# Queries and keys transposed in 32x32 blocks by VectorE, weighing of e moved to GpSimd

## The chip, the cores and the metric

The kernel runs on one core of a Trainium2 chip. The metric is the device time of one execution in microseconds (us). The times shown are those of three runs; the profile is that of one further execution, whose own time stands beside its span.

## What is computed

The reference is an attention with a causal window of 128 tokens and a linear bias, followed by a gated feed-forward layer with a short convolution over the tokens. All arrays are float32.

```python
batch, n_heads, seq, head_dim = (8, 8, 576, 64)          # q, k, v
d_model, d_ff, kernel = 512, 1024, 3

scores = scale * np.matmul(q, k.transpose(0, 1, 3, 2))   # scale 1/8
bias = slopes[:, None, None] * (-np.abs(rel))[None, :, :]
mask = (rel >= 0) & (rel < window)
scores = np.where(mask, scores + bias[None], -1000000000.0)
attn = np.exp(scores - np.max(scores, axis=-1, keepdims=True))
attn = attn / (np.sum(attn, axis=-1, keepdims=True) + 1e-09)
attn_out = np.matmul(attn, v)

x = attn_out, heads side by side, as (8, 576, 512)
h = np.maximum(x @ w_in, 0.0)
conv_out[:, s] = sum over k of conv_w[k] * h[:, s + k - 1]     # zeros outside a sequence
gate = 1.0 / (1.0 + np.exp(-conv_out))
return h * gate @ w_out
```

## The kernel before

The 8 x 576 = 4608 tokens are cut into 36 tiles of 128 tokens, t = 0 to 35, without regard to the ends of the sequences: sequence b begins at token 576b, so a boundary falls at the edge of a tile (tiles 9, 18, 27) or in its middle (tiles 4, 13, 22, 31). The eight heads are taken in two halves u = 0, 1 of four heads (HU).

For a tile, the attention half goes through these steps (the short names are those of the order lists):

- LD: two DMAs (one per piece, where a tile lies in two sequences) bring queries and keys, tokens on partitions, into `rqk`; LV does so for the values, into `rv`. All DMAs are issued by SP's queue.
- Q: TensorE transposes `rqk` in eight 128x128 blocks into PSUM (`pt`, L245); QO: ScalarE copies them to `qkT_all` (L250), which holds three tiles.
- S.u: TensorE makes the scores of a half (`sc`, L287); MA.u.a: VectorE merges, masks and adds the bias, and writes `e` (L308, L316, L319); RM.u: the row maximum (L323).
- X.u.h: ScalarE takes the exponentials of two heads, with their sums (L328).
- N.u: VectorE takes the reciprocal of the sums (L339, L340) and multiplies e by it (L341, one instruction of 128x512).
- T.u: TensorE transposes e into `pa` (L348); RL.u: ScalarE copies it to `rl` (L353); SEL.u: GpSimd cuts it into the side of this tile and that of the tile before (L359, L362).
- AV: TensorE multiplies with the values (L379); XH, XL, XF: the result as a high and a low part in `x` (L390, L394, L408, L410).

The feed-forward half works on chunks of 256 tokens, four steps s to a chunk, two steps to each tile's period: UH (L423, twelve matmuls into `p`), HH (relu, L431), Z and CV (the convolution: L437 on ScalarE, L450 on VectorE), TH (L457), GT (L461), GH (L468), GL (GpSimd, L473), D (L487, twelve matmuls into `o`), OB (store). Where a chunk holds the boundary of two sequences, each CV takes four VectorE instructions in place of two.

The order on every engine is written out by hand: `OPENING` for tiles 0 to 5 with the loading and splitting of the weights (F, CL, RS, V, H, P, W), then `PERIOD` once for each t from 6 to 35, then `TAIL`. A name with a number i in PERIOD means tile t + i or step s + i. Every engine runs its instructions in the order in which the list names them, and waits where an input or a buffer is not ready. The PERIOD of before:

```
S0.0 MA0.0.0 S0.1 GH-1 AV-1 LV2 XH-1 MA0.0.1 XL-1 RM0.0 D-2 OB-2 X0.0.0 X0.0.1 XF-1 UH0.0 HH0.0
MA0.1.0 Z0.0 UH0.1 HH0.1 MA0.1.1 GL-1 UH1.0 RM0.1 X0.1.0 CV0.0 N0.0 Z0.1 UH1.1 T0.0 X0.1.1 HH1.0
CV0.1 TH0 RL0.0 N0.1 HH1.1 Q1 LD3 GT0 SEL0.0 Z1.0 QO1 CV1.0 T0.1 Z1.1 RL0.1 CV1.1 GH0 SEL0.1 TH1 GT1
GL0 D-1 OB-1
```

PSUM for `pt`, `sc`, `pa`, `av` and `p` comes from one pool of five buffers in rotation.

Of the kernel before, what the change touches and what calls it, by code (L numbers as in the profile page):

```python
# [21 lines left out]
def tile_alibi_window_attention_conv_glu(  # L22
# [103 lines left out]

# [108 lines left out]
    def fetch(t, dst, src):  # L235
        for r, b, s, n in segments(t):
            nc.sync.dma_start(out=dst[r : r + n], in_=src[b, :, s : s + n, :].rearrange("h s d -> s h d"))

    def qkT(t, u):
        rqk = raws[t][0]  # L240
        ps = pst.tile([P, 2, NG, P], F32, name=f"pt{t}_{u}", tag="tr")
        for i in range(2):
            for g in range(NG):
                h = u * HU + 2 * g
                nc.tensor.transpose(ps[:, i, g, :], rqk[:, i, h : h + 2, :].rearrange("p h d -> p (h d)"), ident)  # L245
# [91 lines left out]
    def normal(t, u):  # L337
        e, st, pss = sms.pop((t, u))
        nc.vector.tensor_scalar(out=st[:, 2, :], in0=st[:, 1, :], scalar1=1e-9, scalar2=None, op0=ALU.add)  # L339
        nc.vector.reciprocal(out=st[:, 2, :], in_=st[:, 2, :])  # L340
        nc.vector.tensor_tensor(out=e, in0=e, in1=st[:, 2, :].unsqueeze(2).to_broadcast([P, HU, P]), op=ALU.mult)  # L341
        es[t, u] = e

    def attnT(t, u):
        e = es.pop((t, u))
        ps = pst.tile([P, HU, P], F32, name=f"pa{t}_{u}", tag="tr")
        for j in range(HU):
            nc.tensor.transpose(ps[:, j, :], e[:, j, :], ident)  # L348
# [167 lines left out]


# [93 lines left out]
```

## Time and profile before

| | us |
|---|---|
| median of three runs (lowest, highest) | 673.04 (672.59, 673.32) |
| the profiled execution, its own time | 672.56 |
| its span | 670.5 |
| busy: TensorE matmuls, VectorE, ScalarE, GpSimd | 633.5, 514.1, 450.6, 192.5 |

The span is the time from the first to the last record of the profiled execution; the 2.1 us around it belong to its time too. The periodic part (t = 6 to 35) begins at 111.65 us, and the last period begins at 603.71 us. Most periods whose steps hold no boundary take 16.7 us, those that hold one about 17.4 us; three short ones, after a tile that begins a sequence, take 15.8 us.

### The profile page before, as it was taken

What the parts mean: (1) busy time and instruction counts of PE and PEld (TensorE: products, weight loads), DVE (VectorE), ACT (ScalarE), POOL (GpSimd) and SP (SyncE); (2) the same over time, 40 slices, a digit from 0 to 9 for tenths busy, and PEclk for the clock granted to TensorE, in tenths of its full rate; (3) what the DMA queues carried; (4) which work ended last, traced back from release to release, by engine and by line L of the source; (5) the groups of instructions that cost most, each with busy time, mean ns of one, the idle gap of its engine ahead of it and who ended that gap; (6) DMA issues with size and microseconds to landing.
All of it is one profiled execution on the core that took longest, in us unless ns stands there. A gap on an engine that the chain in (4) does not pass through costs nothing.

```text
span 670.5 us, 15774 instructions
## 1 busy us (share of the span) xinstructions
PE 633.5 (94%) x6097; PEld 552.6 (82%) x6097; DVE 514.1 (77%) x1225; ACT 450.6 (67%) x1275; POOL 192.5 (29%) x235
## 2 busy tenths in 40 slices
PE   4679899999999999999999999999999999999996
PEld 3357678988898889888999999988898889888994
DVE  7988997777877788777877788777877888777341
ACT  3768776676767676667676767666776667666452
POOL 2242323332232233223233333322232223223221
PEclk9789999999999999999999999999999999999998
DMA  8753721222222222232502222223232322000000
GB/s 231 199 169 98 171 48 39 57 67 54 73 48 68 61 64 65 48 79 49 126 32 50 80 48 79 50 48 81 48 80 48 81 48 79 18 32 1 32 32 31
DMA packets 120109, 47.16 MB, mean 70 GB/s; under 512 B 113356, under 2 KB 113380, under 8 KB 120036
## 3 DMA queue, kind: packets, MB, share of 16 engines
q1 hardware_dynamic: 120036, 46.17, 26.8%
q8 instruction: 48, 0.79, 0.5%
q14 instruction: 25, 0.20, 0.1%
HBM read 36.72 MB, written 9.44 MB: 69 GB/s over the span
## 4 chain that ended last, share of the span: by engine, by line
PE 67%; DVE 18%; issue 6%; ACT 5%; POOL 2%; DMA 1%; POOLq 0%; SPq 0%; DVEq 0%; ACTq 0%
PE o L487 24%; PE p L423 20%; PE av L379 8%; DVE zp L450 7%; PE sc L287 7%; PE pa L348 4%; PE pt L245 3%; DVE e L341 3%; ACT zp L437 2%; PE pw L200 1%; POOL gl L473 1%; DVE wg L184 1%; DVE z L461 1%; DVE sc L316 1%; DVE wg L181 1%
## 5 line engine op out<-in xcount | busy, mean ns | idle before, releaser
L450 DVE SCALAR_TENSOR_TENSOR zp<-hh,cw,zp 128x256 f32<-128x256 f32 (+7 forms) x384 | 162.0, 422 | 81.6 <-ACT zp L437 72.7
L423 PEld LDWEIGHTS p<-x,wi 128*128 128x128 f32 x1728 | 212.3, 189 | 8.6 <-PE o L487 4.0
L423 PE MATMUL p<-x,wi 128*128 128x258 f32 x1728 | 215.2, 283 | 2.8 <-DVE x L408 2.8
L487 PE MATMUL o<-wo,gh 128*128 128x512 f32 x576 | 188.0, 407 | 1.5 <-ACT gh L468 1.5
L328 ACT ACTIVATE e<-e,st 128x128 f32<-128x128 f32 x288 | 112.1, 391 | 55.4 <-DVE st L323 55.4
L359 POOL TENSOR_SCALAR_AFFINE_SELECT rl<-rl 128x512 f32<-128x512 f32 x64 | 41.4, 647 | 344.5 <-ACT rl L353 344.5
L487 PEld LDWEIGHTS o<-wo,gh 128*128 128x128 f32 x576 | 103.6, 189 | 27.7 <-issue 5.1
L487 PE MATMUL o<-wo,gl 128*128 128x512 f32 x288 | 114.9, 399 | 0.6 <-POOL gl L473 0.6
L473 POOL TENSOR_TENSOR gl<-z,gh 128x512 fp32r<-128x512 f32 x72 | 92.3, 1282 | 53.6 <-ACT gh L468 52.8
L431 ACT ACTIVATE hh<-p 128x258 f32<-128x258 f32 x144 | 55.1, 383 | 45.2 <-PE p L423 45.2
L437 ACT ACTIVATE zp<-hh,cw 128x256 f32<-128x256 f32 x144 | 68.7, 477 | 22.0 <-DVE zp L450 13.7
L461 DVE SCALAR_TENSOR_TENSOR z<-zp,hh 128x512 f32<-128x512 f32 x72 | 49.5, 688 | 28.5 <-ACT zp L457 28.5
L379 PE MATMUL av<-rl,rv 128*64 128x128 f32 x1088 | 69.1, 280 | 1.9 <-POOL rl L362 1.1
L487 PEld LDWEIGHTS o<-wo,gl 128*128 128x128 f32 x288 | 54.5, 189 | 14.2 <-POOL gl L473 1.1
L379 PEld LDWEIGHTS av<-rl,rv 128*64 128x64 f32 x1088 | 60.2, 139 | 6.9 <-issue 3.0
L287 PEld LDWEIGHTS sc<-qkT_all 64*64 64x64 f32 x1792 | 51.7, 136 | 16.8 <-issue 4.7
L319 DVE SCALAR_TENSOR_TENSOR e<-sc,bias 128x256 f32<-128x256 f32 x144 | 61.2, 425 | 4.9
L308 DVE COPY_PREDICATED sc<-m_same,sc 128x256 f32<-128x256 uint8 x144 | 60.5, 420 | 4.9 <-PE sc L287 4.8
L457 ACT ACTIVATE zp<-zp 128x512 f32<-128x512 f32 x72 | 41.9, 582 | 30.2 <-DVE zp L450 18.2
L348 PE MATMUL pa<-ident_r,e 128*128 128x128 f32 x288 | 44.8, 279 | 17.4 <-DVE e L341 12.9
L287 PE MATMUL sc<-qkT_all 64*64 64x128 f32 (+2 forms) x1792 | 59.0, 270 | 2.2 <-DVE e L319 0.8
L362 POOL TENSOR_SCALAR_AFFINE_SELECT rl<-rl 128x512 f32<-128x512 f32 x72 | 46.3, 643 | 48.7 <-ACT rl L353 37.0
(65 smaller groups left out, 626.3 us busy)
## 6 DMA issues: line engine op xcount, KB each, us to landing
out_dram<-ob SPq DMA_DIRECT2D x36, 256.0 KB, 2.2
rqk<-in_q_dram SPq DMA_DIRECT2D x32, 256.0 KB, 3.6
rqk<-in_k_dram SPq DMA_DIRECT2D x32, 256.0 KB, 3.9
rv<-in_v_dram SPq DMA_DIRECT2D x32, 256.0 KB, 3.2
wst<-in_moe_w_in_dram SPq DMA_DIRECT2D x8, 512.0 KB, 5.5
wst<-in_moe_w_out_dram SPq DMA_DIRECT2D x8, 512.0 KB, 4.0
rqk<-in_q_dram SPq DMA_DIRECT2D x8, 128.0 KB, 3.3
rqk<-in_k_dram SPq DMA_DIRECT2D x8, 128.0 KB, 3.6
```

Of the source, the lines that this page charges most:

```text
L287: nc.tensor.matmul(strip(pss[a][qs, g, :], [to for to, _ in run]), qkT_all[rows, 0, u, g, base + c * QW : base + (c + 1) * QW], strip(qkT_ ...
L308: nc.vector.copy_predicated(out=s_all.rearrange("p g (c w) -> p g c w", w=QW), mask=m_same.rearrange("p (c w) -> p c w", w=QW).unsqueeze(1 ...
L319: nc.vector.scalar_tensor_tensor(out=heads, in0=s_all, scalar=-0.125, in1=b, op0=ALU.mult, op1=ALU.add)
L328: nc.scalar.activation(out=e[:, j, :], in_=e[:, j, :], func=AF.Exp, bias=st[:, 0, j : j + 1], scale=-1.0, accum_out=st[:, 1, j : j + 1],)
L348: nc.tensor.transpose(ps[:, j, :], e[:, j, :], ident)
L379: nc.tensor.matmul(ps[a * D : (a + 1) * D, u * NG + g], vraw[tt][:, u * HU + j], rl[:, side, j], start=n == 0, stop=n == len(sides) - 1,)
L423: nc.tensor.matmul(ps[:, :XW], a[:, cc, f * P : (f + 1) * P], x[:, cc, :], start=n == 0, stop=n == last)
L437: nc.scalar.activation(out=zps[s][:, ff, :], in_=hhs[s][:, ff, 1 : 1 + CW], func=AF.Copy, scale=cw[:, 1, f : f + 1])
L450: nc.vector.scalar_tensor_tensor(out=z[:, ff, a:cut], in0=hh[:, ff, a + kk : cut + kk], scalar=cw[:, kk, f : f + 1], in1=z[:, ff, a:cut], ...
L461: nc.vector.scalar_tensor_tensor(out=zgs[s], in0=zps.pop(s), scalar=1.0, in1=hhs.pop(s)[:, :, 1 : 1 + CW], op0=ALU.add, op1=ALU.mult)
L473: nc.gpsimd.tensor_tensor(out=gl, in0=zgs.pop(s), in1=as32(gh), op=ALU.subtract)
L487: nc.tensor.matmul(oos[c][m], g[:, ff, ms], w[:, f, :], start=f == 0 and n == 0, stop=f == NFC - 1 and n == 2)
```

## The change

Three things change together.

1. The weighing. N.u keeps the two short VectorE instructions on the sums; the multiplication of e becomes a step of its own, M.u, on GpSimd. It stands right behind N.u in the lists.
2. The transposes. Tiles 0 to 8 (the first two sequences) are loaded and transposed as before, but with four DMAs of 4 heads each in place of two. From tile 9 on there are no LD, Q and QO. LB brings a whole sequence of queries and keys by eight DMAs into an area of `arena`, 32 partitions x 72 rows of 128 bytes each, so that 32x32 blocks lie below one another; QV then transposes them on VectorE straight into `qkT_all`, with two instructions to a tile (four where a tile lies in two sequences). Six such loads are issued, in the periods t = 6, 8, 13, 17, 22 and 26, for the sequences 2 to 7. Two areas take turns; they use the space that `rqk` and the weights' staging buffers had, all of it now one tensor, `arena`.
3. The order and the heads. Head h now lies at place (a, u, g) = (h // 4, h % 4 // 2, h % 2), for the bias and for the matmuls with the values. In PERIOD, MA0.1.0 moves ahead of XL-1 and XF-1 on VectorE, and RM0.0 ahead of XL-1; QV1 stands behind RM0.1.

```diff
-        rqk = apool.tile([P, 2, H, D], F32, name=f"rqk{t}", tag="rqk", bufs=3)
-        for dst, src in ((rqk[:, 0], q), (rqk[:, 1], k)):
-            fetch(t, dst, src)
+        if t >= NAT:                       # NAT = 2 * S // P = 9
+            return
+        rqk = arena[:, (t % NRQ) * RQ : (t % NRQ + 1) * RQ].rearrange(...)
+        for i, src in enumerate((q, k)):
+            for a in range(2):
+                fetch(t, rqk[:, i, a], src[:, a * HU : (a + 1) * HU])
...
+    def loadb(t):
+        for b in range(2, B):
+            if t == (FIRST if b == 2 else NAT - 1 if b == 3 else ((b - 1) * S - 1) // P):
+                kb = kbs[b] = arena[:, KB_AT[b % 2] : KB_AT[b % 2] + KB].rearrange("p (i g s) -> p i g s", i=2, s=S)
+                for i, src in enumerate((q, k)):
+                    for a in range(2):
+                        for c in range(2):
+                            rows = slice(a * D + c * 32, a * D + (c + 1) * 32)
+                            nc.sync.dma_start(
+                                out=kb[rows, i].rearrange("r g (n d) -> r (g n) d", d=32),
+                                in_=src[b, a * HU : (a + 1) * HU, :, c * 32 : (c + 1) * 32].rearrange(
+                                    "h (n r) d -> r (h n) d", r=32),
+                            )
+
+    def qkV(t):
+        if t < NAT:
+            return
+        slot = t % SLOTS
+        for i in range(2):
+            for r, b, s0, n in segments(t):
+                nc.vector.transpose(
+                    out=qkT_all[:, i].rearrange("p u g s -> p (u g) s")[:, :, slot * P + r : slot * P + r + n],
+                    in_=kbs[b][:, i, :, s0 : s0 + n],
+                )
...
-        nc.vector.tensor_tensor(out=e, in0=e, in1=st[:, 2, :].unsqueeze(2).to_broadcast([P, HU, P]), op=ALU.mult)
-        es[t, u] = e
+        es[t, u] = e, st
+
+    def weigh(t, u):
+        e, st = es[t, u]
+        nc.gpsimd.tensor_tensor(out=e, in0=e, in1=st[:, 2, :].unsqueeze(2).to_broadcast([P, HU, P]), op=ALU.mult)
...
     PERIOD = """
-    S0.0 MA0.0.0 S0.1 GH-1 AV-1 LV2 XH-1 MA0.0.1 XL-1 RM0.0 D-2 OB-2 X0.0.0 X0.0.1 XF-1 UH0.0 HH0.0
+    S0.0 MA0.0.0 S0.1 GH-1 AV-1 LV2 LB0 XH-1 MA0.0.1 RM0.0 MA0.1.0 XL-1 XF-1 D-2 OB-2 X0.0.0 X0.0.1 UH0.0 HH0.0
...
```

The places that matter are shown for tile 21, whose period begins at 365.40 us in the profile before. TensorE's queue around the two transposes of e (`pa`), before:

```order
L423 MATMUL p_1_4923<-x_4186,wi_122 128x258
L348 MATMUL pa_0_4936<-ident_r,e_0_4797 128x128 x4
L245 MATMUL pt_0_4954<-ident_r,rqk_4502 128x128 x4
L245 MATMUL pt_1_4959<-ident_r,rqk_4502 128x128 x4
L348 MATMUL pa_1_4977<-ident_r,e_1_4878 128x128 x4
L487 MATMUL o_0_4614<-wo_123,gh_4819 128x512
```

and in the changed kernel:

```order
L464 MATMUL p_1_4757<-x_4044,wi_121 128x258 x2
L464 MATMUL p_1_4757<-x_4044,wi_122 128x258
L390 MATMUL pa_0_4770<-ident_r,e_0_4627 128x128 x4
L390 MATMUL pa_1_4796<-ident_r,e_1_4675 128x128 x4
L528 MATMUL o_0_4463<-wo_123,gh_4649 128x512
```

The eight transposes of the next tile's queries and keys stood between the two transposes of e; now the second follows the first at once.

GpSimd's queue over the same period, before:

```order
L473 TENSOR_TENSOR gl_4759<-z_4738,gh_4758 128x512
L473 TENSOR_TENSOR gl_4820<-z_4764,gh_4819 128x512
L359 AFFINE_SELECT rl_0_4948<-rl_0_4948 128x512
L362 AFFINE_SELECT rl_0_4948<-rl_0_4948 128x512
L359 AFFINE_SELECT rl_1_4983<-rl_1_4983 128x512
L362 AFFINE_SELECT rl_1_4983<-rl_1_4983 128x512
```

and in the changed kernel:

```order
L514 TENSOR_TENSOR gl_4589<-z_4570,gh_4588 128x512
L514 TENSOR_TENSOR gl_4650<-z_4594,gh_4649 128x512
L384 TENSOR_TENSOR e_0_4627<-e_0_4627,st_0_4628 128x512
L384 TENSOR_TENSOR e_1_4675<-e_1_4675,st_1_4676 128x512
L401 AFFINE_SELECT rl_0_4782<-rl_0_4782 128x512
L404 AFFINE_SELECT rl_0_4782<-rl_0_4782 128x512
```

The two weighings stand between the last GL and the cuts of rl. VectorE's queue from the second row maximum on, before:

```order
L323 TENSOR_REDUCE st_1_4879<-e_1_4878 128x4
L450 SCALAR_TENSOR_TENSOR zp_4882<-hh_4876,cw,zp_4882 128x255
L450 SCALAR_TENSOR_TENSOR zp_4882<-hh_4876,cw,zp_4882 128x256
L339 TENSOR_SCALAR st_0_4798<-st_0_4798 128x4
L340 RECIPROCAL st_0_4798<-st_0_4798 128x4
L341 TENSOR_TENSOR e_0_4797<-e_0_4797,st_0_4798 128x512
L450 SCALAR_TENSOR_TENSOR zp_4882<-hh_4876,cw,zp_4882 128x255
L450 SCALAR_TENSOR_TENSOR zp_4882<-hh_4876,cw,zp_4882 128x256
L339 TENSOR_SCALAR st_1_4879<-st_1_4879 128x4
L340 RECIPROCAL st_1_4879<-st_1_4879 128x4
L341 TENSOR_TENSOR e_1_4878<-e_1_4878,st_1_4879 128x512
```

and in the changed kernel:

```order
L362 TENSOR_REDUCE st_1_4676<-e_1_4675 128x4
L244 STREAM_TRANSPOSE qkT_all<-arena 128x4x64 x4
L491 SCALAR_TENSOR_TENSOR zp_4712<-hh_4710,cw,zp_4712 128x255
L491 SCALAR_TENSOR_TENSOR zp_4712<-hh_4710,cw,zp_4712 128x256
L378 TENSOR_SCALAR st_0_4628<-st_0_4628 128x4
L379 RECIPROCAL st_0_4628<-st_0_4628 128x4
L491 SCALAR_TENSOR_TENSOR zp_4712<-hh_4710,cw,zp_4712 128x255
L491 SCALAR_TENSOR_TENSOR zp_4712<-hh_4710,cw,zp_4712 128x256
L378 TENSOR_SCALAR st_1_4676<-st_1_4676 128x4
L379 RECIPROCAL st_1_4676<-st_1_4676 128x4
```

The block transposes (four half-size ones here, since tile 22 lies in two sequences) come in ahead of the convolution, and the two multiplications of e are gone from this queue.

More of the change, by code (lines that the diff above doesn't have):

```diff
@@ L121, in tile_alibi_window_attention_conv_glu @@
         slope = 2.0 ** (-8.0 * (h + 1) / H)
+        a, u, g = h // HU, h % HU // 2, h % 2
         nc.vector.tensor_scalar(
-            out=bias[:, h, :], in0=dist, scalar1=slope, scalar2=None, op0=ALU.mult
+            out=bias[:, u * HU + 2 * g + a, :], in0=dist, scalar1=slope, scalar2=None, op0=ALU.mult
         )
@@ L147, in weight_blocks @@
             yield moe_w_out[f * P : (f + 1) * P, :], [w[:, f, :] for w in wo]
-    wpool = ctx.enter_context(tc.tile_pool(name="wpool", bufs=3))
-    NST = 6
+    NST, NWG, NRQ = 6, 3, 3
+    RQ, ST, WG, KB = 2 * H * D, 2 * WB, WB, 2 * HU * S
+    arena = cpool.tile([P, NRQ * RQ + NST * ST + NWG * WG], F32, name="arena")
+    KB_AT = (NRQ * RQ + NST * ST + NWG * WG - KB, 0)
+    assert 2 * KB <= NRQ * RQ + NST * ST + NWG * WG
     blocks = list(weight_blocks())
     NW = 3 * NFC
-    wst, wgs, pws = {}, {}, {}
+    wst, wgs, pws, wseen = {}, {}, {}, []
     def fetch_weight(b):
-        st = wpool.tile([P, WB, 2], U32, name=f"wst{b}", tag="wst", bufs=NST)
+        at = NRQ * RQ + (b % NST) * ST
+        st = arena[:, at : at + ST].bitcast(U32).rearrange("p (n t) -> p n t", t=2)
         if blocks[b] is None:
@@ L171, in w_rebias @@
     def w_rebias(b):
-        g = wpool.tile([P, WB], U32, name=f"wg{b}", tag="wg")
+        at = NRQ * RQ + NST * ST + (len(wseen) % NWG) * WG
+        wseen.append(b)
+        g = arena[:, at : at + WB].bitcast(U32)
         wgs[b] = g[:NW, :P] if blocks[b] is None else g
@@ L210, in tile_alibi_window_attention_conv_glu @@
     SLOTS = 3
+    FIRST = 6
     NG = HU // 2
+    NAT = 2 * S // P
+    kbs = {}
+    def loadb(t):
[9 more added lines that the diff above has]
+                                in_=src[b, a * HU : (a + 1) * HU, :, c * 32 : (c + 1) * 32].rearrange(
+                                    "h (n r) d -> r (h n) d", r=32
+                                ),
+                            )
[9 more added lines that the diff above has]
+                )
     qkT_all = cpool.tile([P, 2, 2, NG, SLOTS * P], F32, name="qkT_all")
@@ L225, in load @@
     def load(t):
-        rqk = apool.tile([P, 2, H, D], F32, name=f"rqk{t}", tag="rqk", bufs=3)
-        for dst, src in ((rqk[:, 0], q), (rqk[:, 1], k)):
-            fetch(t, dst, src)
-        raws[t] = [rqk]
+        if t >= NAT:
+            return
+        rqk = arena[:, (t % NRQ) * RQ : (t % NRQ + 1) * RQ].rearrange(
+            "p (i g a d) -> p i a g d", i=2, a=2, d=D
+        )
+        for i, src in enumerate((q, k)):
+            for a in range(2):
+                fetch(t, rqk[:, i, a], src[:, a * HU : (a + 1) * HU])
     def loadv(t):
@@ L239, in qkT @@
     def qkT(t, u):
-        rqk = raws[t][0]
         ps = pst.tile([P, 2, NG, P], F32, name=f"pt{t}_{u}", tag="tr")
@@ L243, in qkT @@
             for g in range(NG):
-                h = u * HU + 2 * g
-                nc.tensor.transpose(ps[:, i, g, :], rqk[:, i, h : h + 2, :].rearrange("p h d -> p (h d)"), ident)
+                at = (t % NRQ) * RQ + (i * HU + 2 * u + g) * P
+                nc.tensor.transpose(ps[:, i, g, :], arena[:, at : at + P], ident)
         pts[t, u] = ps
@@ L374, in av @@
             rl = rls.pop((t, u))
-            for g in range(NG):
+            for a in range(2):
                 for n, (side, tt) in enumerate(sides):
-                    for a in range(2):
-                        j = 2 * g + a
+                    for g in range(NG):
                         nc.tensor.matmul(
-                            ps[a * D : (a + 1) * D, u * NG + g],
-                            vraw[tt][:, u * HU + j],
-                            rl[:, side, j],
+                            ps[g * D : (g + 1) * D, 2 * a + u],
+                            vraw[tt][:, a * HU + 2 * u + g],
+                            rl[:, side, 2 * g + a],
                             start=n == 0,
@@ L503, in qk @@
     def qk(t):
-        for u in range(2):
-            qkT(t, u)
+        if t < NAT:
+            for u in range(2):
+                qkT(t, u)
     def qk_out(t):
-        for u in range(2):
-            qkT_out(t, u)
+        if t < NAT:
+            for u in range(2):
+                qkT_out(t, u)
     TILE = {
@@ L515, in tile_alibi_window_attention_conv_glu @@
         "X": lambda t, u, h: exps(t, u, range(2 * h, 2 * h + 2)),
-        "N": normal, "T": attnT, "RL": attn_out, "SEL": select, "AV": av, "XH": x_hi, "XL": x_lo, "XF": xfin,
+        "N": normal, "M": weigh, "LB": loadb, "QV": qkV, "T": attnT, "RL": attn_out, "SEL": select, "AV": av, "XH": x_hi, "XL": x_lo, "XF": xfin,
     }
@@ L542, in tile_alibi_window_attention_conv_glu @@
     LD0 F0 LD1 LV0 F1 F2 F3 F4 LD2 LV1 F5 Q0 CL0 QO0 S0.0 S0.1 RS0 Q1 MA0.0.0 MA0.1.0 MA0.1.1 MA0.0.1
-    QO1 RM0.1 V0 F6 X0.1.1 S1.0 CL1 CL2 MA1.0.0 RM0.0 S1.1 X0.1.0 X0.0.0 MA1.0.1 X0.0.1 RS2 N0.1 CL3
-    RM1.0 N0.0 H0 V2 T0.1 X1.0.0 RS1 T0.0 CL4 RL0.1 MA1.1.0 P0 V1 F7 F8 LD3 LV2 RS3 H2 X1.0.1 P2 W2
-    RL0.0 MA1.1.1 RM1.1 SEL0.1 H1 SEL0.0 W0 P1 Q2 V3 F9 X1.1.1 AV0 W1 RS4 X1.1.0 N1.0 N1.1 CL7 V4 F10
+    QO1 RM0.1 V0 F6 X0.1.1 S1.0 CL1 CL2 MA1.0.0 RM0.0 S1.1 X0.1.0 X0.0.0 MA1.0.1 X0.0.1 RS2 N0.1 M0.1 CL3
@@ L546, in tile_alibi_window_attention_conv_glu @@
+    RM1.0 N0.0 M0.0 H0 V2 T0.1 X1.0.0 RS1 T0.0 CL4 RL0.1 MA1.1.0 P0 V1 F7 F8 LD3 LV2 RS3 H2 X1.0.1 P2 W2
+    RL0.0 MA1.1.1 RM1.1 SEL0.1 H1 SEL0.0 W0 P1 Q2 V3 F9 X1.1.1 AV0 W1 RS4 X1.1.0 N1.0 M1.0 N1.1 M1.1 CL7 V4 F10
     T1.0 H3 QO2 CL5 P3 T1.1 RL1.0 S2.0 RL1.1 MA2.0.0 S2.1 RS5 SEL1.1 MA2.0.1 MA2.1.0 CL6 RM2.0 SEL1.0
-    MA2.1.1 X2.0.0 AV1 Q3 V5 F11 RS6 X2.0.1 H4 QO3 V6 F12 LD4 LV3 P4 W4 CL10 XH0 RM2.1 N2.0 S3.0 XH1
-    X2.1.1 X2.1.0 H6 H5 MA3.0.0 T2.0 CL8 N2.1 MA3.0.1 RL2.0 T2.1 XL1 S3.1 W3 P5 P6 RM3.0 RL2.1 XL0 RS8
+    MA2.1.1 X2.0.0 AV1 Q3 V5 F11 RS6 X2.0.1 H4 QO3 V6 F12 LD4 LV3 P4 W4 CL10 XH0 RM2.1 N2.0 M2.0 S3.0 XH1
@@ L549, in tile_alibi_window_attention_conv_glu @@
+    X2.1.1 X2.1.0 H6 H5 MA3.0.0 T2.0 CL8 N2.1 M2.1 MA3.0.1 RL2.0 T2.1 XL1 S3.1 W3 P5 P6 RM3.0 RL2.1 XL0 RS8
     CL9 MA3.1.0 SEL2.0 SEL2.1 XF1 RS7 W6 V7 F13 AV2 Q4 X3.0.0 W5 XF0 XH2 V8 F14 CL11 XL2 H7 QO4 X3.0.1
-    P7 MA3.1.1 XF2 RS9 UH0.0 N3.0 T3.0 W7 H8 HH0.0 CL12 Z0.0 RM3.1 UH1.0 X3.1.0 X3.1.1 HH1.0 V9 F15 P8
-    UH1.1 CL14 RS11 CV0.0 UH0.1 RS10 RL3.0 H9 W8 N3.1 HH0.1 T3.1 HH1.1 S4.0 V11 V10 F16 LD5 LV4 LD6 LV5
+    P7 MA3.1.1 XF2 RS9 UH0.0 N3.0 M3.0 T3.0 W7 H8 HH0.0 CL12 Z0.0 RM3.1 UH1.0 X3.1.0 X3.1.1 HH1.0 V9 F15 P8
@@ L552, in tile_alibi_window_attention_conv_glu @@
+    UH1.1 CL14 RS11 CV0.0 UH0.1 RS10 RL3.0 H9 W8 N3.1 M3.1 HH0.1 T3.1 HH1.1 S4.0 V11 V10 F16 LD5 LV4 LD6 LV5
     LD7 Z0.1 RL3.1 CV0.1 H11 TH0 H10 MA4.0.0 P9 SEL3.0 RS12 GT0 GH0 SEL3.1 UH2.0 Z1.0 HH2.0 MA4.0.1
-    CV1.0 RM4.0 P11 CL16 P10 AV3 LV6 W9 Z1.1 UH2.1 V12 W11 X4.0.1 X4.0.0 H12 CV1.1 P12 TH1 N4.0 CL13 GT1
+    CV1.0 RM4.0 P11 CL16 P10 AV3 LV6 W9 Z1.1 UH2.1 V12 W11 X4.0.1 X4.0.0 H12 CV1.1 P12 TH1 N4.0 M4.0 CL13 GT1
     XH3 GL0 W10 Z2.0 GH1 S4.1 XL3 CV2.0 CL15 UH3.0 HH2.1 Z2.1 MA4.1.0 HH3.0 RS13 CV2.1 D0 MA4.1.1 GL1
@@ L555, in tile_alibi_window_attention_conv_glu @@
     RS15 TH2 W12 Q5 LD8 GT2 Q6 RS14 XF3 RM4.1 Z3.0 V13 UH3.1 QO5 V14 HH3.1 T4.0 CV3.0 H13 D1 QO6 X4.1.0
-    Z3.1 X4.1.1 S5.0 V15 N4.1 H14 MA5.0.0 RL4.0 P13 H15 P14 T4.1 SEL4.0 RL4.1 SEL4.1 CV3.1 MA5.0.1 W13
+    Z3.1 X4.1.1 S5.0 V15 N4.1 M4.1 H14 MA5.0.0 RL4.0 P13 H15 P14 T4.1 SEL4.0 RL4.1 SEL4.1 CV3.1 MA5.0.1 W13
     GH2 W14 S5.1 P15 W15 GL2 MA5.1.0 AV4 LV7 TH3 XH4 RM5.0 GT3 X5.0.1 X5.0.0 XL4 D2 XF4 UH4.0 MA5.1.1
-    GH3 RM5.1 RS16 HH4.0 V16 X5.1.0 N5.0 Z4.0 H16 UH5.0 UH4.1 CV4.0 P16 X5.1.1 HH4.1 N5.1 GL3 Z4.1 HH5.0
+    GH3 RM5.1 RS16 HH4.0 V16 X5.1.0 N5.0 M5.0 Z4.0 H16 UH5.0 UH4.1 CV4.0 P16 X5.1.1 HH4.1 N5.1 M5.1 GL3 Z4.1 HH5.0
@@ L563, in tile_alibi_window_attention_conv_glu @@
     PERIOD = """
-    S0.0 MA0.0.0 S0.1 GH-1 AV-1 LV2 XH-1 MA0.0.1 XL-1 RM0.0 D-2 OB-2 X0.0.0 X0.0.1 XF-1 UH0.0 HH0.0
-    MA0.1.0 Z0.0 UH0.1 HH0.1 MA0.1.1 GL-1 UH1.0 RM0.1 X0.1.0 CV0.0 N0.0 Z0.1 UH1.1 T0.0 X0.1.1 HH1.0
-    CV0.1 TH0 RL0.0 N0.1 HH1.1 Q1 LD3 GT0 SEL0.0 Z1.0 QO1 CV1.0 T0.1 Z1.1 RL0.1 CV1.1 GH0 SEL0.1 TH1 GT1
+    S0.0 MA0.0.0 S0.1 GH-1 AV-1 LV2 LB0 XH-1 MA0.0.1 RM0.0 MA0.1.0 XL-1 XF-1 D-2 OB-2 X0.0.0 X0.0.1 UH0.0 HH0.0
+    Z0.0 UH0.1 HH0.1 MA0.1.1 GL-1 UH1.0 RM0.1 QV1 X0.1.0 CV0.0 N0.0 M0.0 Z0.1 UH1.1 T0.0 X0.1.1 HH1.0
+    CV0.1 TH0 RL0.0 N0.1 M0.1 HH1.1 Q1 LD3 GT0 SEL0.0 Z1.0 QO1 CV1.0 T0.1 Z1.1 RL0.1 CV1.1 GH0 SEL0.1 TH1 GT1
     GL0 D-1 OB-1
```

3 lines of the change are left out of this document (1 added, 2 removed).

## The prediction

> **What bounds the kernel now.** I read the page first, for which engine carries the chain that ended last.
>
> ```profile
> PE 633.5 (94%) x6097; PEld 552.6 (82%) x6097; DVE 514.1 (77%) x1225; ACT 450.6 (67%) x1275; POOL 192.5 (29%) x235
> PE 67%; DVE 18%; issue 6%; ACT 5%; POOL 2%; DMA 1%; POOLq 0%; SPq 0%; DVEq 0%; ACTq 0%
> ```
>
> TensorE carries two thirds of the chain, so work taken from it should count, unless something else is close behind. The chain in order of time shows one period of tile 21, whose steps hold no boundary:
>
> ```profile
> 371.86 5.74 PE p L423 x48
> 377.60 0.44 PE pa L348 x4
> 378.04 0.87 PE pt L245 x8
> 378.91 0.44 PE pa L348 x4
> 379.34 2.80 PE o L487 x12
> 382.14 1.50 PE sc L287 x32
> ```
>
> It is TensorE without a gap, and the change takes out the 0.87 us of `pt` between the two transposes of e. What counts is therefore how long before its transpose the second e is ready. The timeline of the same period says so (start, duration, engine, line, tiles; in brackets the idle time before and who ended it):
>
> ```profile
> 369.53 0.69 DVE L394 TENSOR_TENSOR x<-av,x 128x512 fp32r<-128x512 f32 x1 [1.11 <-ACT x L390]
> ...
> 374.26 1.01 DVE L450 SCALAR_TENSOR_TENSOR zp<-hh,cw,zp 128x255 f32<-128x255 f32 x2 [1.06 <-ACT zp L437]
> 374.76 0.39 ACT L431 ACTIVATE hh<-p 128x258 f32<-128x258 f32 x1 [0.54 <-PE p L423]
> ...
> 375.38 0.18 DVE L340 RECIPROCAL st<-st 128x4 f32<-128x4 f32 x1
> ...
> 375.82 0.46 ACT L437 ACTIVATE zp<-hh,cw 128x256 f32<-128x256 f32 x1
> ...
> 376.31 1.01 DVE L450 SCALAR_TENSOR_TENSOR zp<-hh,cw,zp 128x255 f32<-128x255 f32 x2
> ...
> 377.43 0.18 DVE L340 RECIPROCAL st<-st 128x4 f32<-128x4 f32 x1
> 377.44 0.60 PE L348 MATMUL pa<-ident_r,e 128*128 128x128 f32 x4
> 377.64 0.69 DVE L341 TENSOR_TENSOR e<-e,st 128x512 f32<-128x512 f32 x1
> 378.07 0.59 ACT L353 COPY rl<-pa 128x512 f32<-128x512 f32 x1
> 378.73 0.63 POOL L359 TENSOR_SCALAR_AFFINE_SELECT rl<-rl 128x512 f32<-128x512 f32 x1 [9.88 <-ACT rl L353]
> 378.75 0.60 PE L348 MATMUL pa<-ident_r,e 128*128 128x128 f32 x4
> ```
>
> The second e is weighed by 378.33 and transposed at 378.75: 0.42 us ahead, no more. Its weighing is the end of a run that hangs on TensorE: p's second half lets ScalarE's relu go at 374.76, behind it in ScalarE's order come two exponentials, the L437 of 375.82, two exponentials; VectorE's convolution waits for that L437 (376.31), and the reciprocal ends at 377.61.
>
> Where the steps hold a boundary, the convolution has four instructions, and TensorE already waits (period of tile 30; the wait stands in brackets):
>
> ```profile
> 527.98 0.48 ACT L437 ACTIVATE zp<-hh,cw 128x256 f32<-128x256 f32 x1
> ...
> 528.81 1.52 DVE L450 SCALAR_TENSOR_TENSOR zp<-hh,cw,zp 128x128 f32<-128x128 f32 x4
> ...
> 530.44 0.18 DVE L340 RECIPROCAL st<-st 128x4 f32<-128x4 f32 x1
> ...
> 531.49 0.63 PE L348 MATMUL pa<-ident_r,e 128*128 128x128 f32 x4 [0.47 <-DVE e L341]
> ```
>
> The groups by line give the prices and the counts:
>
> ```profile
> L473 POOL TENSOR_TENSOR gl<-z,gh 128x512 fp32r<-128x512 f32 x72 | 92.3, 1282 | 53.6 <-ACT gh L468 52.8
> L341 DVE TENSOR_TENSOR e<-e,st 128x512 f32<-128x512 f32 x72 | 49.8, 692 | 2.5
> L323 DVE TENSOR_REDUCE st<-e 128x4 f32<-128x512 f32 x72 | 49.0, 681 | 1.1
> L362 POOL TENSOR_SCALAR_AFFINE_SELECT rl<-rl 128x512 f32<-128x512 f32 x72 | 46.3, 643 | 48.7 <-ACT rl L353 37.0
> L450 DVE SCALAR_TENSOR_TENSOR zp<-hh,cw,zp 128x191 f32<-128x191 f32 x32 | 13.5, 422 | 1.1
> L316 DVE COPY_PREDICATED_SCALAR sc<-m_half,neg 128x256 f32 x16 | 7.8, 488 | 0.6
> ```
>
> Six cut widths of 32 instructions each make 48 convolutions of four, so 24 steps or 12 periods hold a boundary; the other 18 of the 30 do not.
>
> **The transposes that leave TensorE.** 27 tiles (9 to 35) lose 0.87 us each, 23.5 us, if nothing else ends the wait for the second e. ScalarE loses two copies of pt a tile; it does not set the end there.
>
> **The weighing on GpSimd.** It is a multiplication of two 128x512 inputs, the second a broadcast. The trace has GpSimd's two-input instruction in that size, L473 at 1.282 us (the same to 0.02 us over the run); its one-input cut, L362, takes 0.643. I take 1.28 and keep 0.64 as the cheap end; an end above, 1.5, would be an estimate of L473 slowed by a sixth.
>
> [...]
>
> Handing over costs twice: from the copy's end at 378.66 GpSimd started at 378.73, so 0.07 us in; out I take what VectorE's e costs TensorE, from the chain in a boundary period:
>
> ```profile
> 582.13 0.70 DVE e L341
> 582.83 0.14 issue
> 582.97 0.63 PE pa L348 x4
> ```
>
> So without a boundary the second transpose can start at 377.61 + 0.07 + 1.28 + 0.14 = 379.10, where TensorE alone would be there at 377.88 and was there at 378.75 before. TensorE waits 1.2 us: the 0.87 is gone, and 0.35 us more. Behind the waiting transposes stand the twelve matmuls of D, then the next scores; all shift with it. Over 18 periods, 6.3 us.
>
> With a boundary, VectorE loses the first L341, so its convolution starts when its L437 is done, at 528.46 instead of 528.81; the reciprocal ends 0.33 earlier, at 530.29, and the transpose can start at 530.29 + 0.07 + 1.28 + 0.14 = 531.78 against 531.49: 0.29 us later, over 12 periods 3.5 us.
>
> The first e has its reciprocal at 375.56, so it is there at 377.05, ahead of 377.44. On GpSimd the second weighing ends at 378.96, and the cuts of the first half, which began at 378.73, start 0.23 us later; with the second half's cuts and one L473 they need 2.6 + 1.3 us and end by 382.9. The next period would start near 382.4 and AV comes 1.5 us into it, so GpSimd's queue holds nobody up. GL stands ahead of the weighings and is done long before (9.88 us idle).
>
> **The block transposes on VectorE.** No row shows such an instruction. The nearest are VectorE's passes over 128x512 float32 between SBUF tiles, 0.68 to 0.69 us (L323, L341); I take 0.69, and 1.28 (L473, another engine's price for the size) as the dear end, 0.5 as the cheap one. [...] Two for a tile are 1.38 us, as much as the two L341 that go. They lie ahead of the convolution: the brackets show VectorE idle there for 1.06 us and, ahead of L394, for 1.11 us, which the new order fills with RM0.0 and MA0.1.0. 2.17 us hold 1.38. QV is needed by the scores of the next period only.
>
> That cover is missing in 9 tiles of the periodic part that have one more mask (L316, four instructions, 1.95 us): the tiles that begin a sequence, hold its end or follow that. For tile 18, VectorE's timeline shows no idle time between
>
> ```profile
> 317.35 0.69 DVE L461 SCALAR_TENSOR_TENSOR z<-zp,hh 128x512 f32<-128x512 f32 x1 [0.72 <-ACT zp L457]
> ...
> 328.25 0.18 DVE L340 RECIPROCAL st<-st 128x4 f32<-128x4 f32 x1
> ```
>
> so there QV's 1.38 comes in, 0.69 of the first L341 goes out, and up to 0.7 at the start is won since L457 and L461 of the period before no longer stand behind ScalarE's copies of pt. That leaves 0 to 0.7 us; I take 0.3 each, 2.7 us.
>
> **The loads.** Before, tiles needed two DMAs each; six sequences now need eight DMAs of 2304 rows.
>
> ```profile
> q1 hardware_dynamic: 120036, 46.17, 26.8%
> L237 SPq DMA_DIRECT2D rqk<-in_q_dram x40: 368/611/1585, 0.8 to 556.2; - x40
> ...
> DMA to landing us min/median/max: 2.6/3.6/7.6
> ```
>
> 26.8% of 16 engines' 670.5 us over 120036 packets are 24 ns a packet; a sequence has 18432, so 28 us if all engines share. SP's issue is 0.6 us for 1024 rows; at 1.4 us for 2304 the eight take 11 us, beside the transfers. The first sequence is issued in period 6 and read in the middle of period 8, some 40 us later; the others have four to five periods, over 60 us. Values and stores queue behind them for up to 28 us; values are loaded two periods ahead of AV and a chunk's store has two periods until its buffer is reused. I take 0; the dear end is a rival below.
>
> **The opening.** VectorE is rid of 12 x 0.69 = 8.3 us at best, and each of the 12 e comes up to 0.65 us later, 7.8 us at worst. The list of waits says that TensorE seldom waited there for e:
>
> ```profile
> PE pa L348 <- DVE e L341: 12.9, 14, 6.7
> ```
>
> 12 of the 14 are the boundary periods with some 0.47 us, one is 6.7. The first loads are four DMAs in place of two, about 1 us later. I take 0, with 3 us either way.
>
> **The sum.** 6.3 + 3.5 + 2.7 = 12.5 us on the profiled execution's 672.56: 685.1. That execution lies 0.5 us under the median of the runs, 673.04, so 685.5 for a median; I say 685.
>
> **The rivals.**
>
> - GpSimd weighs as quickly as it cuts. With 0.64 the second transpose starts at 378.46 without a boundary (0.29 earlier than before, 18 times) and at 531.14 with one (0.35, 12 times): 5.2 + 4.2 us won, and with the 2.7 lost 666. The point from which it decides is 0.93 us a weighing. Against it stands L473, two inputs as well. This is the other side: faster. Chance 0.10.
> - The 23.5 us come through whole (650), because the chain to e could run ahead of TensorE. Against it: the relu at 374.76 waited for p. Chance 0.03.
> - GpSimd need not read the broadcast anew for each element, and its price lies half-way between its two rows, at 0.96. Without a boundary 0.03 us are then lost, with one 0.03 won, and with the 2.7 it is 675 to 676. Only the shape of the second input speaks for it. [...] Chance 0.10, half of it for the 2.7 staying away too, which is no change.
> - The block transposes are dear. At 1.28 us two take 2.56 against 2.17 of room: 0.4 us more in 21 periods, 8 us, and in the nine masked ones 1.2 us more, 11 us: 704. Chance 0.12.
> - The loads come late. At 7.6 us a transfer, one after another, a sequence takes 61 us; VectorE then stands at QV for 20 us in period 8, with the convolution and N behind it and so TensorE: about 705. The 24 ns a packet speak against it. Chance 0.05.
>
> **The numbers.** My forecast, slower by 8 to 16 us (681 to 689), has 0.58; the rivals above have 0.40 and 0.02 is left for what I do not see. From 674 to 698 lie the forecast, most of the half-way price, and the milder half of the two dear rivals, some 0.8. A measurement of this kernel tells a change from none at about 0.2%, 1.3 us. Faster by more than that: the first two rivals, 0.13 and 0.01 of the unseen; within: 0.05, half of the third; slower: the rest, 0.81.
>
> **What would show it.** In the profile after, each period's second `pa` has a wait of about 1.2 us on GpSimd's e, and the chain runs p, relu, L437, convolution, reciprocal, weighing, pa. GpSimd's new group has 72 instructions of 1.28 us. VectorE's transposes are 48 of 0.69 and 12 of some 0.4. No wait on a DMA of `arena` after the opening. Periods without a boundary are 17.05 us long, against 16.7. A weighing under 0.93 us makes the sign wrong; transposes over 1.1 us, or a wait of VectorE for arena, make it too low.

## The result and the profile after

The changed kernel takes 682.84 us (median of four runs, 681.73 to 682.89) against 673.18 us before (four runs too); the ratio is 1.014, with a 95% interval of 1.0122 to 1.0157. It is slower by 9.7 us, where 685 was forecast. The profiled execution took 681.73 us, its span is 680.0 us.

The page of the changed kernel, busy time and the chain that ended last:

```profile
PE 615.8 (91%) x5881; PEld 529.3 (78%) x5881; DVE 509.6 (75%) x1213; ACT 421.9 (62%) x1221; POOL 265.6 (39%) x307
DVE 39%; PE 36%; ACT 11%; issue 8%; POOL 4%; DMA 1%; SPq 0%; POOLq 0%; DVEq 0%; ACTq 0%
```

TensorE lost 17.7 us of busy time, yet the span grew by 9.5: its share of the chain fell from 67% to 36%, VectorE's rose from 18% to 39%. The work left the engine that set the end, and the end moved to the others. The waits by pair of engines say where (total, times, longest):

```profile
PEld pa L390 <- POOL e L384: 50.7, 41, 5.7
...
PE pa L390 <- POOL e L384: 40.8, 36, 5.6
...
PE p L464 <- DVE x L449: 7.3, 7, 1.9
```

TensorE waits for the weighed e, as forecast; the weight load and the matmul of the same transpose both show that wait. The third row, which had 2.8 us before, was not forecast to grow. The groups of the two new operations, beside GpSimd's other two-input group:

```profile
L514 POOL TENSOR_TENSOR gl<-z,gh 128x512 fp32r<-128x512 f32 x72 | 92.3, 1282 | 42.9 <-ACT gh L509 41.9 <-PE o L528 0.3
L384 POOL TENSOR_TENSOR e<-e,st 128x512 f32<-128x512 f32 x72 | 75.1, 1044 | 283.8 <-DVE st L379 229.0 <-ACT e L367 40.2 <-ACT arena L181 8.9
L244 DVE STREAM_TRANSPOSE qkT_all<-arena 128x512 f32<-128x512 f32 x48 | 31.1, 686 | 0.0
```

Tile 21's timeline in the changed kernel has the forecast order of events at the second e:

```profile
383.56 0.18 DVE L379 RECIPROCAL st<-st 128x4 f32<-128x4 f32 x1
...
383.88 1.04 POOL L384 TENSOR_TENSOR e<-e,st 128x512 f32<-128x512 f32 x1 [1.01 <-DVE st L379]
...
384.97 0.66 PE L390 MATMUL pa<-ident_r,e 128*128 128x128 f32 x4 [0.82 <-POOL e L384]
```

The reciprocal ends at 383.74, GpSimd starts 0.14 us later, the transpose 0.05 us after its end. The hand-over in and out is 0.19 us; 0.21 was taken.

The 30 periods fall into three kinds (a period is measured from the start of one tile's scores to the next one's): 9 plain ones, 12 that hold a boundary, and 9 masked ones (tiles 9, 13, 14, 18, 22, 23, 27, 31, 32). Of the last, I call 9, 13, 23, 27 and 31 odd: there a new chunk begins, whose first matmuls need XF of the same period. Tiles 9, 13, 27 and 31 follow a period with a boundary and agree to 0.02 us; tile 23 does not, and it went from 16.71 to 17.35, by as much as the even tile 14.

| period, us | before | after |
|---|---|---|
| plain (tile 20) | 16.71 | 16.84 |
| with a boundary (tile 30) | 17.36 | 17.46 |
| masked, odd behind a boundary (tile 13) | 17.41 | 18.49 |
| masked, even (tile 14) | 16.71 | 17.35 |
| all to tile 35's start, the gain or loss | | 1.8 plain, 1.0 boundary, 8.0 masked |

With 0.5 us in the opening and 1.7 won at the end, that is the span's 9.5.

### The profile page after: what moved, and what is told of

The parts are those of the page before. It is cut to its first block, busy times and chain, and to the rows that moved or that the text cites. A ratio compares the mean times of both kernels' runs of the same rounds, so it can differ in the third digit from the quotient of the medians.

```text
span 680.0 us, 15406 instructions
## 1 busy us (share of the span) xinstructions
PE 615.8 (91%) x5881; PEld 529.3 (78%) x5881; DVE 509.6 (75%) x1213; ACT 421.9 (62%) x1221; POOL 265.6 (39%) x307
## 4 chain that ended last, share of the span: by engine, by line
DVE 39%; PE 36%; ACT 11%; issue 8%; POOL 4%; DMA 1%; SPq 0%; POOLq 0%; DVEq 0%; ACTq 0%
DVE zp L491 15%; PE o L528 14%; PE p L464 9%; PE av L420 5%; ACT zp L478 5%; PE sc L326 4%; DVE e L358 4%; DVE sc L347 3%; DVE sc L355 3%; DVE st L362 3%; DVE z L502 3%; DVE qkT_all L244 2%; ACT zp L498 2%; POOL e L384 2%; PE pa L390 2%
## 5 line engine op out<-in xcount | busy, mean ns | idle before, releaser
L384 POOL TENSOR_TENSOR e<-e,st 128x512 f32<-128x512 f32 x72 | 75.1, 1044 | 283.8 <-DVE st L379 229.0
L390 PE MATMUL pa<-ident_r,e 128*128 128x128 f32 x288 | 46.5, 285 | 41.2 <-POOL e L384 40.8
L390 PEld LDWEIGHTS pa<-ident_r,e 128*128 128x128 f32 x288 | 32.4, 142 | 51.4 <-POOL e L384 50.7
L401 POOL TENSOR_SCALAR_AFFINE_SELECT rl<-rl 128x512 f32<-128x512 f32 x64 | 41.2, 644 | 46.9 <-ACT rl L395 46.8
```

The source lines that it names most:

```text
L384: nc.gpsimd.tensor_tensor(out=e, in0=e, in1=st[:, 2, :].unsqueeze(2).to_broadcast([P, HU, P]), op=ALU.mult)
```

## The experiments

Ten kernels were run. Theory A is the forecast's: the second e gates TensorE, and VectorE has no room in the masked periods. The rivals are named in the expectations. Each ratio is to the kernel before on the same chip.

**e1: the weighing back on VectorE.**

```diff
-        nc.gpsimd.tensor_tensor(out=e, in0=e, in1=st[:, 2, :]...
+        nc.vector.tensor_tensor(out=e, in0=e, in1=st[:, 2, :]...
```

> The changed kernel with the two weighings back on VectorE at the same places (transposes in blocks stay). Theory A (the second e gates TensorE, and VectorE has no room in tiles with one more mask): in the 9 plain periods the second e comes 0.39 us earlier than with GpSimd's 1.04 us, so they fall from 16.85 to about 16.45 us; the 12 boundary periods stay within 0.1; the 9 masked ones get 0.7 us of VectorE work ahead of the second e and grow by 0.3 to 1.0. Together 686 us (681 to 692). Rival B (GpSimd's weighing is the whole reason why the 23.5 us did not come): without it the time falls to 650 to 665 us. Rival C (the loads of 128-byte rows cost the time): unchanged, 682 to 683.

Measured: 691.84 us, 1.0268 (1.0242 to 1.0295), at the upper edge of A's range. Plain periods fell to 16.46 (tile 20), as A says; tile 14 grew to 17.77, tile 13 to 18.85, tiles 9 and 27 to 20.16, tile 31 to 19.81. In tile 9 the granted clock (the share of its full clock that TensorE gets) was 0.85 in the mean from 175 to 185.5 us, and 1.00 over the same tile of the changed kernel. Half of the boundary periods grew by 0.3 to 0.5 us (tile 30 to 17.9), where A had less than 0.1. With the transposes on VectorE, the move to GpSimd is worth 9 us: VectorE cannot carry the transposes and both weighings together. Rival B falls.

**e2: the weighing alone.** The kernel before, with the one line on GpSimd and M behind N in the lists.

> The kernel before with the weighing alone moved to GpSimd; loads, transposes on TensorE and the order stay as before. Theory A: second e 0.1 us later in plain and boundary periods (21 x 0.1 = 2 us lost), VectorE rid of 0.69 us ahead of it in the 9 masked ones (0.4 to 0.8 us won each, 3.6 to 7): 669.5 us (666 to 673). Rival B (the weighing is the loss): about 682. Rival C: 672 to 674, no change.

Measured: 672.33 us, 0.9995 (0.9979 to 1.0012): no change. Plain 16.85, boundary 17.45, as after the whole change; tiles 9 and 13, odd and masked, fell to 16.97 and 16.96. The time is within A's range and within C's too; the periods tell the two apart, since they moved the ways that A says. What the plain and boundary periods lose, the odd masked ones win only in part: in the profiled execution the periodic part (to tile 35's start) is 1.2 us longer and the opening 0.6, and the end is 1.8 shorter, where the clock of before fell (see The ends).

**e3: VectorE's order as before.** XL-1 ahead of RM0.0, XF-1 and MA0.1.0 behind, in PERIOD; the rest as changed.

> The changed kernel with VectorE's order of the merges and of XL, XF as before (XL-1 ahead of RM0.0, XF-1 behind it, MA0.1.0 later). Theory A: the new order fills VectorE's wait ahead of XL; without it 1.1 us of room go, the transposes push the convolution in boundary and masked periods by 0.3 to 0.8 us: 690 us (686 to 696). Rival D (the new order itself is what makes the masked periods of odd tiles 1.07 us longer, since XF, which lets the next chunk's matmuls go, now stands behind one more merge): those five periods shrink by 0.5 to 1 us and the rest stays: 677 to 680.

Measured: 685.18 us, 1.0172 (1.0129 to 1.0216). In its profile tile 13 takes 18.16 where the changed kernel takes 18.49, tile 14 17.51 against 17.35, boundary periods up to 0.15 more; tiles 27 and 31 took 19.7, where the granted clock fell to 0.50 (492 to 494 and 564 to 566 us). Neither expectation holds: the order moves single periods by up to 0.3 us, either way.

**e6: without the block transposes.** `qkV` returns at once; from tile 9 on scores are made of older queries and keys.

> The changed kernel without VectorE's block transposes: from tile 9 on the scores use what lies in qkT_all from earlier tiles; the loads are still issued. Theory A (the transposes cost nothing where VectorE idled, and their length where it is full): plain periods stay at 16.85 and boundary ones at 17.45 us; the masked ones fall, those of tiles 14, 22, 23, 32 from 17.35 to 16.85 and those of 9, 13, 27, 31 from 18.49 to about 17.8; together 677.5 us (675 to 680). Rival D (the new order of XL and XF makes the 9, 13, 27, 31 long): these stay at 18.4, together 680. Rival B' (the transposes are the whole loss): 673 or less.

Measured: 682.47 us, 1.0145 (1.0115 to 1.0175). Tiles 14, 22 and 32 fell to 16.86, 16.84 and 16.85, as A says; plain and boundary ones stayed; tiles 9, 13 and 31 stayed at 18.50, 18.51 and 18.53, as D says. Tile 23, odd as well, stayed too, at 17.42, where A had it fall. Rival B' falls. In this profile tile 27 took 20.00, with the clock at 0.50 from 482 to 484 us; and the last ten matmuls took 4.0 us, 1.4 longer than the changed kernel's, so that the time hardly shows what the even masked tiles won.

The loads were still issued here, and plain, boundary and even masked periods (16.86, 17.44, 16.85) are those of e2 (16.85, 17.45, 16.85), which has the old loads: rival C, that the loads cost the time, falls as well.

So e2, e3 and e6 together make a square for the odd masked tile 13, all with the weighing on GpSimd (e2 still has the transposes on TensorE; "without" means none on VectorE):

| tile 13, us | without transposes | with transposes |
|---|---|---|
| VectorE's order as before | 16.96 (e2) | 18.16 (e3) |
| the new order | 18.51 (e6) | 18.49 (changed) |

Either of the two costs 1.2 to 1.6 us there, and the second adds 0.3 us at most. The chains in order of time show two mechanisms. In e6:

```profile
240.38 0.42 DVE e L358
240.80 0.61 DVE x L435
241.41 0.02 issue
241.43 0.19 DVE x L449
241.62 0.14 issue
241.76 1.70 PE p L464 x12
```

x stands behind three merges of 1.3 us and a row maximum, and TensorE's first matmul of the chunk waits for it. In e3:

```profile
243.90 0.69 DVE st L362
244.58 1.21 DVE qkT_all L244 x2
245.79 0.39 DVE zp L491
```

here x comes in time (the chunk's first matmul starts 6.30 us into the period and waits for nothing), and VectorE passes from the row maximum through the transposes to the convolution without a pause.

**e7: a full second operand.** `in1=bias[:, :HU]` in place of the broadcast sums, which leaves the normalisation out.

> The changed kernel with GpSimd's second input a full 128x512 tile (the bias of four heads) in place of the broadcast sums; it leaves the normalisation out. If the broadcast makes the weighing cheaper than GL's 1.28 us, the group takes 1.28 us here and the time is some 5 to 7 us above the changed kernel's (second e 0.24 us later in 21 to 30 periods); if the difference lies in GL's output of another type, it stays at 1.04 us and the time at 682 to 683.

One execution, 701.07 us; its time says nothing on the price, since the weighing no longer waits for the reciprocal and the granted clock was 0.963 in the mean. The group does:

```profile
L384 POOL TENSOR_TENSOR e<-e,bias 128x512 f32<-128x512 f32 x72 | 93.1, 1293 | 256.6 <-ACT e L367 252.7 <-PE p L464 3.8
```

1.293 against 1.044 us: it is the broadcast that makes the weighing cheaper, by 0.25 us, and not the type of the output.

**e4: two exponentials ahead of a relu.**

```diff
-    Z0.0 UH0.1 HH0.1 MA0.1.1 GL-1 UH1.0 RM0.1 QV1 X0.1.0 CV0.0
+    Z0.0 UH0.1 MA0.1.1 GL-1 UH1.0 RM0.1 QV1 X0.1.0 HH0.1 CV0.0
```

> The changed kernel with one move in ScalarE's order: the first two exponentials of the second half ahead of the relu of p's second half (HH0.1). Theory A: the run from that relu to the second e gets shorter by two exponentials, 0.8 us; plain periods fall from 16.85 to 16.3 us (9 x 0.5), boundary ones from 17.45 by 0.3 (12 x 0.3), masked ones, where VectorE is full, stay: 682.8 - 8 = 675 us (672 to 679). Rival B' (only VectorE's fullness counts): 682 to 683, no change.

Measured: 683.4 us, 1.0154 (1.0126 to 1.0181): nothing won in sum, outside A's range. Plain periods fell to 16.41 and 16.43 (tiles 20 and 21), as A says. Boundary ones stayed at 17.45, where A had 0.3 less. Their timeline (tile 30) shows what I had missed:

```profile
535.21 1.49 DVE L491 SCALAR_TENSOR_TENSOR zp<-hh,cw,zp 128x128 f32<-128x128 f32 x4
...
536.79 0.48 ACT L478 ACTIVATE zp<-hh,cw 128x256 f32<-128x256 f32 x1 [0.59 <-DVE st L378]
...
537.30 1.53 DVE L491 SCALAR_TENSOR_TENSOR zp<-hh,cw,zp 128x128 f32<-128x128 f32 x4 [0.33 <-ACT zp L478]
```

ScalarE, free early, starts the second half's product of `zp` only as the first half's convolution ends at 536.70. Both halves lie in one PSUM tile (`zp`, L477), which I take for the reason; no run gives them a tile each. The run in boundary periods goes convolution, product, convolution, whatever the exponentials do. And tile 18 took 19.30 us; the stretches around it (length, busy time of PE, PEld, DVE, ACT and POOL, granted clock) show TensorE's clock:

```profile
332.00:334.00 2.00, 1.01 (x9) 0.80 (x8) 1.57 (x7) 1.79 (x7) 1.04 (x1) 1.00 0.00 0
334.00:336.00 2.00, 1.04 (x8) 0.76 (x7) 0.70 (x2) 1.65 (x4) 1.63 (x2) 0.96 0.02 4
336.00:338.00 2.00, 2.00 (x6) 1.55 (x5) 1.03 (x3) 0.58 (x3) 0.00 (x0) 0.50 0.00 0
338.00:340.00 2.00, 2.00 (x7) 1.44 (x6) 1.24 (x3) 1.53 (x3) 1.50 (x2) 0.68 0.01 4
340.00:342.00 2.00, 2.00 (x56) 1.76 (x56) 1.21 (x4) 0.62 (x1) 1.28 (x2) 1.00 0.00 0
```

After four us with TensorE half busy (1.01 and 1.04 us of 2), it gets 0.50 of its clock from 336 to 338 us and 0.68 in the two us behind. The lower clock does not always follow: in the changed kernel's tile 27 TensorE was busy for 2.13 of 4 us (480 to 484 us), and the clock stayed at 1.00, in the two us behind as well.

**e8: one weighing on each engine.** The kernel before, without block transposes and in its old order; the first half is weighed on GpSimd, the second on VectorE.

```diff
-        nc.vector.tensor_tensor(out=e, in0=e, in1=st[:, 2, :]...      (in N)
+        eng = nc.vector if u else nc.gpsimd                            (in M, behind N)
+        eng.tensor_tensor(out=e, in0=e, in1=st[:, 2, :]...
```

> The kernel before with the first half's weighing on GpSimd and the second half's on VectorE as before; transposes on TensorE, order as before. Theory A: the first e had 1.15 us to spare, so GpSimd's 1.04 us cost nothing; VectorE is rid of 0.69 us ahead of the second e. Plain periods stay at 16.7 us, boundary ones fall by 0.35 us (from 17.37 to 17.0, 12 times), masked ones by 0 to 0.4: 668 us (665 to 670). Rival B (any weighing on GpSimd costs): 673 or more.

Measured: 666.95 us, 0.992 (0.9897 to 0.9943): faster than both kernels, and within A's range. Boundary periods fell to 17.04 (tile 30), plain ones stayed at 16.71, tile 13 fell to 17.34. The second e of tile 30, whose scores begin at 514.58 in e8:

```profile
527.21 0.18 DVE L340 RECIPROCAL st<-st 128x4 f32<-128x4 f32 x1
527.42 0.69 DVE L346 TENSOR_TENSOR e<-e,st 128x512 f32<-128x512 f32 x1
528.26 0.63 PE L352 MATMUL pa<-ident_r,e 128*128 128x128 f32 x4 [0.15 <-DVE e L346]
```

It comes 13.68 us into the period; before it was 531.49 - 517.49 = 14.00. Of the 5.8 us between the spans of the two profiles, the periodic part wins 4.2; 1.8 lie in the end, where the clock of before fell, and the opening loses 0.3.

**e9: e8 with e4's move.**

> e8 with the first two exponentials of the second half ahead of the relu of p's second half in ScalarE's order. Theory A: plain periods stay at 16.7 us, where TensorE is without a gap; in boundary periods the run goes through the convolution, not through these exponentials, so little is won: 0 to 2 us below e8. Rival: the exponentials decide in the boundary periods too: 4 us below e8.

Measured: 667.17 us, 0.9925 (0.9901 to 0.9948), as e8. The exponentials are not in the run that decides here.

**e10: the changed kernel with e8's division.** The block transposes stay on VectorE.

> The changed kernel (block transposes on VectorE) with the second half weighed on VectorE, the first on GpSimd. It asks whether the 0.87 us taken from TensorE pay once the second e is not late. Theory A: plain periods fall to 16.45 us (the second e then comes 0.28 us ahead of its place before, and no more of the 0.87 shows), boundary ones to 17.05, as in e8, since their run passes VectorE's convolution; masked ones stay 0.6 to 1.1 above before, since the transposes or the new order fill VectorE there: 9 x 0.27 won and 9 x 0.8 lost against e8's 667: 672 (669 to 678). Rival F (with the second e in time the transposes' gain comes through): 650 to 660.

Measured: 683.75 us, 1.0151 (1.0126 to 1.0176). Plain periods 16.45, and half of the boundary ones 17.05, as A says; the others of those (the even tiles) took 17.5 to 17.6 and the masked ones 17.45 to 18.7, with 20.0 at tiles 13 and 31. At tile 13 the 48 matmuls into p took 7.54 us (6.02 in the changed kernel); at tile 31 the clock was 0.59 from 552 to 554 us and 0.56 from 554 to 556. In the even tile 30 the chain lies on VectorE nearly without a break for 9 us, from z through merges, maximum and transposes into the convolution: with the second weighing back, VectorE is full there too, which A had not counted. Rival F falls; A's sum was 12 us too low.

**e11: e10 with e4's move.**

> e10 with the first two exponentials of the second half ahead of the relu of p's second half. Theory A: the second e comes another 0.5 us earlier in plain periods, so that TensorE is nearly without a gap there at 15.9 to 16.0 us (9 x 0.5 won against e10), boundary and masked ones as in e10: 667 to 673. Rival F: 645 to 655.

Measured: 679.46 us, 1.0100 (1.0062 to 1.0137), above A's range. Plain periods fell to 16.03 and 16.02 (tiles 20 and 21). In tile 21 TensorE takes both halves' transposes without a wait between them:

```profile
380.70 1.25 PE L391 MATMUL pa<-ident_r,e 128*128 128x128 f32 x8
```

So 0.69 of the 0.87 us taken from TensorE do come through when e is early enough; in e9, with the same two moves and the transposes still on TensorE, plain periods stayed at 16.71. But only 9 of 30 periods are plain, and in the others VectorE's run is longer than before (tile 13 18.54, tile 14 17.45, tile 30 17.60).

## Why the prediction was right, and where its terms were off

**Right: the 0.87 us do not come.** TensorE's transposes went, and the second e was late in their place. e11's plain periods show the counter-case, in which they come.

**Right: the place of the second e.** The working put the second reciprocal 12.03 us into tile 21's period and the late transpose 13.70; they stand at 12.04 and 13.45. TensorE's wait there is 0.82 us where 1.2 was forecast, and the plain period 16.84 where 17.05 was: both are shorter mainly because the weighing was priced 0.24 us too high.

**Too dear: the weighing.** The term of 1.28 us measured 1.044; with a full tile as second operand it measured 1.293 (e7). The chosen row was right for its form and wrong for this one. The half-way rival was right that the broadcast lowers the price, though at 0.96 it went too far; how GpSimd reads the broadcast, no run shows. With 1.04 the working gives 0.11 us for a plain period and 0.05 for a boundary one; measured were 0.13 (tile 20) and 0.10 (tile 30), and the sums of 6.3 and 3.5 shrink together to 2.6 for all 30 periods. The turning point of 0.93 us a weighing was that of a plain period alone; with the working's own 2.7 us and 0.99 for a boundary period, its sum turns at 0.86.

**Too cheap: the masked periods.** For these the working has 2.7 us, and with the weighing at 1.04 another 1.0 as their share of it; 8.0 were measured. Two steps failed. The working let up to 0.7 us be won at the start of the period because ScalarE's copies of pt go. In the changed kernel's tile 18 VectorE still waits for ScalarE's L498 ahead of z, 0.72 us as before:

```profile
321.38 0.69 DVE L502 SCALAR_TENSOR_TENSOR z<-zp,hh 128x512 f32<-128x512 f32 x1 [0.72 <-ACT zp L498]
```

This z began 0.48 us after the tile's scores (0.74 before), so 0.26 were won; e2, which still has the copies of pt, shows the same 0.48. And the new order was counted as filling VectorE's wait ahead of XL; that in odd masked periods XL then stands behind three masked merges, with TensorE's next chunk waiting for it, was not seen. In tile 13, before:

```profile
237.87 6.00 PE L423 MATMUL p<-x,wi 128*128 128x258 f32 x48 [0.36 <-DVE x L408]
```

and in the changed kernel:

```profile
241.09 6.02 PE L464 MATMUL p<-x,wi 128*128 128x258 f32 x48 [1.40 <-DVE x L449]
```

This wait is 1.04 us longer, nearly all of what the period lost. The chain of tile 13 in the changed kernel carries it:

```profile
240.14 0.61 DVE x L435
240.75 0.02 issue
240.77 0.19 DVE x L449
240.96 0.14 issue
241.09 6.02 PE p L464 x48
```

e6 shows that this alone, and e3 that the transposes alone, would have made these periods long.

**Right: the transposes' price.** 0.686 us for 0.69; the half-size ones 0.41 for 0.4.

**Right: the loads are hidden.** No wait on a load of the block transposes appears. SP's issue of 2304 rows took 1.47 us in the median (1.4 taken), and the slowest landed in 5.7:

```profile
L231 SPq DMA_DIRECT2D arena<-in_q_dram x24: 519/1465/2542, 116.1 to 465.3; - x24
...
DMA to landing us min/median/max: 4.0/4.6/5.7
```

**The ends.** The opening cost 0.5 us (0 taken). The 1.7 us won at the end are mostly the last ten matmuls, 4.01 us before and 2.61 after. The change does no work there; the granted clock differs. Before, it was 0.52 from 662 to 664 us and 0.63 from 664 to 666; in the changed kernel it was 1.00 from 673 to 677. No term of the sum has this, so for the forecast it is luck; why the clock falls in the end of some executions and not of others stays open. The end of the chain, of before:

```profile
662.39 4.01 PE o L487 x10
```

and of the changed kernel:

```profile
673.72 2.61 PE o L528 x10
```

So the time agrees to 2.2 us in part by luck, because terms were off in opposite directions: 7 us too much for the weighing, 4 too little for the masked periods beside it, 1 too little for the plain and boundary ones (half of it in tile 19, behind a masked one), and the 0.5 and 1.7 of the ends.

## What to carry to other kernels

Before work is taken off the engine that sets the end, read how long before its use the next input is ready there; 0.42 us ahead of the second transpose decided over 0.87 us of freed matmuls. An operation moved to a slower engine (this one takes 1.04 us on GpSimd, 0.69 on VectorE) belongs where there is such a lead: moved in both halves, the weighing cost 1.2 us of the periodic part (e2), and in the first half alone, with no block transposes, it won 4.2 us (e8). And price the rare form of a loop body by itself: nine of thirty periods, with one more mask, brought 8.0 of the 10.8 us.

## What the runs showed of the hardware

GpSimd's multiplication of 128x512 float32 by a broadcast takes 1.044 us, by a full tile 1.293. TensorE's granted clock fell to 0.50 for two us, with 0.68 in the next two, after four us in which it was busy for 2.05 (tile 18 in e4); the tile took 2 us more than the same tile of the changed kernel. In tiles 27 and 31 of e3 and tile 27 of e6, with 19.7 to 20.0 us, the clock fell to 0.50 as well, in tile 31 of e10, with 20.0, to 0.56. After 2.13 us busy of four in tile 27 of the changed kernel it stayed at 1.00; whether the gaps brought the clock down was not settled.
